# Writing out the order of three attention batches between an expert's matmul steps, and moving half of the query copies to ScalarE

## The chip, the core and the metric

The kernel runs on one NeuronCore of a Trainium2 chip. The core has a matrix engine (TensorE, "PE" in the profile, with its weight loads as "PEld"), a vector engine (VectorE, "DVE"), a scalar engine (ScalarE, "ACT"), a general-purpose engine (GpSimd, "POOL") and a sync engine ("SP") that here only issues transfers. [...] Matmul results land in PSUM, which the kernel uses as eight banks; everything else lies in SBUF. The metric is the time of one execution on the device, in microseconds; smaller is better.

## The reference

Two layers follow each other.

1. Attention with sorted blocks: batch 4, 8 heads, 768 positions, head size 64. A small matrix per head, 8 by 8, is normalised five times by rows and columns (Sinkhorn); it mixes the eight blocks of 96 keys and the eight blocks of 96 values. Each block of 96 queries then attends to its own mixed block.

```python
k_sorted = einsum('bhij,bhjcd->bhicd', P, k_b)
v_sorted = einsum('bhij,bhjcd->bhicd', P, v_b)
scores = scale * q_b @ k_sorted^T          # per block of 96
attn = softmax(scores)
x = attn @ v_sorted                        # laid out as 3072 tokens of 512
```

2. A layer of eight experts over all 3072 tokens. The logits `x @ w_gate` are made into a routing matrix P of 3072 by 8 by eight rounds of row and column normalisation over all tokens, and then

```python
for e in range(8):
    out += P[:, e:e+1] * (maximum(x @ w1[e], 0) @ w2[e])     # 512 -> 1024 -> 512
```

So no expert's output can be weighted before the logits of all four batches are there, but an expert's two matmuls need only the tokens that they multiply.

## The kernel before, in words

The span of 671.6 us has four stretches.

- **0 to 40 us**: the Sinkhorn matrices, and the attention of batch 0.
- **40 to 130 us**: the attention of batches 1, 2 and 3 (the loop of lines 515 to 543), each beside the dense first expert (`expert0`, line 418) of the batch ahead of it. This is the stretch that the change touches.
- **130 to 172 us**: the rest of expert 0 (`last_dense`), beside the routing's rounds (`balance`) and the first tiles of expert 1.
- **172 to 671 us**: experts 1 to 7, each by seven products in place of eight (Strassen), with sums of inputs, weights and hidden values made by GpSimd.

In the second stretch a batch is worked on by head pairs 0 to 3 (`hp`), in steps named by a letter:

- `q` (`queries`): six (twelve in batch 1) transposes of a pair's queries into one PSUM bank, then one copy of 128x768 to SBUF. Batch 1 transposes 64 columns at a time from `qt` (line 171); batches 2 and 3 first have GpSimd put a pair's queries side by side (`qr`, line 176, two buffers) and transpose 128 columns at a time (line 180). The copy is line 184 (ScalarE, batch 0) or line 186 (VectorE, batches 1 to 3).
- `k` (`keys`): the block mixing of the keys as matmuls (line 196) into two banks, and two VectorE copies (line 202).
- `s` (`scores`): 16 matmuls (line 220) into four banks, and four exponentials on ScalarE (line 234).
- `d` (`sums`): the softmax denominators by matmuls with ones (line 302) into two banks; the reciprocal is made on ScalarE by a logarithm (line 305) and an exponential (line 307).
- `m` (`mix`): attention times values (line 315) into two banks, and on VectorE the product with the reciprocal into the token tile `xtT` (line 318).
- `l` (`logits`): the gate's logits of the batch (line 331), `l0` for three of the four contraction blocks, `l3` for the last, then a copy into `glog` (line 335).

`sort_values` mixes the values of the batch: eight matmuls (line 147), eight copies (line 149, ScalarE and VectorE by turns) and eight transfers through which the mixed values change partitions (line 158, SP and GpSimd queues by turns). It is a generator that stops after every second head.

`expert0` is also a generator. A hidden step is four matmuls of 384 columns (line 397) and a rectifier on ScalarE (line 403) or VectorE (line 400). Half of an output tile is four matmuls of 512 columns (line 410); after the second half the tile is copied out (line 415), by ScalarE for tiles below 6 and by VectorE above. Batch 0 has 20 such steps left in this stretch, batches 1 and 2 have 28 each (8 hidden, 6 output, 8 hidden, 6 output).

What sets the order: TensorE's instructions are pinned to the order in which the program writes them. `weave(a, b, na, nb)` writes them by taking `na` visits to the attention generator and spreading `nb` expert steps between them evenly. The copies and other work of ScalarE, VectorE and GpSimd are mostly not pinned in batches 1 to 3; a scheduler places them on their engine when the program is built. The transfers of the next batch's `v`, `k`, `q` (line 80, GpSimd queue), the building of its mixing matrix `Rt` (line 134), and in batch 2 the load of expert 1's `w1` (line 89) and its sums (line 440) are pinned in the order of GpSimd.

All PSUM tiles of this stretch come from one pool of eight banks (`pa`, line 511), tag "bank". Buffers that hold several visits' work: `qTs` 4, `kTs` 3, `atp` 12 (three pairs' exponentials; in batch 1 the fourth pair uses the `qr` buffers), `recip` six slots in `osbl`.

Of the kernel before, what the change touches and what calls it, by code (L numbers as in the profile page):

```python
# [20 lines left out]
def mkap(t, dims, off=0):  # L21
    return bass.AP(tensor=t.tensor, offset=t.offset + off, ap=dims)
# [3 lines left out]
def kernel(  # L26
# [11 lines left out]
    nc = tc.nc  # L38
    B, H, S, D = 4, 8, 768, 64
# [19 lines left out]
    pin = tc.keep_in_program_order  # L59
# [12 lines left out]
    def load_batch(bb, parts):  # L72
        for d, name in ((vt, "vt"), (kt, "kt"), (qt, "qt")):
            d[bb] = kvp.tile([128, 8, 384], BF16, name=name, bufs=2)
        load_rest(bb, parts)

    def load_rest(bb, parts):
        for x, l0, n in parts:
            d, src = {"v": (vt, v), "k": (kt, k), "q": (qt, q)}[x]
            pin(nc.gpsimd.dma_start(  # L80
                out=d[bb][:, l0:l0 + n, :],
                in_=src[bb, l0:l0 + n].rearrange("h (p kk) d -> p h (kk d)", kk=6)))
# [4 lines left out]
    def load_w1(e):  # L87
        w1t[e] = wp.tile([128, 4, F], BF16, name="w1e")
        pin(nc.gpsimd.dma_start(out=w1t[e],
                                in_=moe_w1[e].rearrange("(kk k) f -> k kk f", k=128)))  # L90
# [39 lines left out]
    def build_r(bb, eng, n):  # L130

        Rt[bb] = perp.tile([128, 8, 8, 16], BF16, name=f"R{bb % 2}")
        for h in range(0, 8, n):
            ins = eng.tensor_tensor(
                out=mkap(Rt[bb], [Rt[bb].ap[0], [16, 8 * n], [1, 16]], off=h * 128),
                in0=mkap(Pb, [Pb.ap[0], [1, 8 * n], [0, 16]], off=(bb * 8 + h) * 8),
                in1=mkap(mask16, [mask16.ap[0], [0, 8 * n], [1, 16]]),
                op=ALU.mult)
            if eng is nc.gpsimd:
                pin(ins)  # L140
            yield


    def sort_values(bb, bank, n=8, h0=0):
        for h in range(h0, n):
            vps = bank([128, 384], F32)
            pin(nc.tensor.matmul(vps, Rt[bb][:, h].rearrange("p i c -> p (i c)"),  # L147
                                 vt[bb][:, h, :], start=True, stop=True))
            (nc.vector.tensor_copy if bb == 0 and h in (3, 5, 7) or bb and h % 2 else
             nc.scalar.copy)(  # L150
                vs[:, :, h, 0:64], vps.rearrange("p (kk d) -> p kk d", d=64))
            if h % 2:
                yield

        for i in range(NB if n == 8 else 0):
            eng = ((nc.sync, nc.gpsimd, nc.scalar)[i % 3] if bb == 0 else
                   nc.gpsimd if i % 2 else nc.sync)
            (pin if bb == 0 else lambda ins: ins)(eng.dma_start(
                out=mkap(vsbt[bb % 2], [[VW, 96], [1, 520]], off=i * 520),
                in_=vs[16 * i:16 * i + 16].rearrange("p kk h d -> p kk (h d)")))  # L160

    qT, kT, og = {}, {}, {}

    def queries(bb, hp, bank):

        qps = bank([128, 6, 128], BF16)
        if bb < 2:

            for kk in range(6):
                for h in range(2):  # L170
                    pin(nc.tensor.matmul(qps[64 * h:64 * h + 64, kk, :],
                                         qt[bb][:, 2 * hp + h, kk * 64:kk * 64 + 64],
                                         Ibig, is_transpose=True, start=True, stop=True))
        else:
            qr = sp.tile([128, 6, 2, 64], BF16, name="qr", bufs=2)
            nc.gpsimd.tensor_copy(
                qr.rearrange("p kk h d -> p h kk d"),
                qt[bb][:, 2 * hp:2 * hp + 2].rearrange("p h (kk d) -> p h kk d", d=64))
            for kk in range(6):
                pin(nc.tensor.matmul(qps[:, kk, :], qr[:, kk].rearrange("p h d -> p (h d)"),  # L180
                                     Ibig, is_transpose=True, start=True, stop=True))
        qT[bb, hp] = sp.tile([128, 128, 6], BF16, name="qTs", bufs=4)
        if bb == 0:
            pin(nc.scalar.copy(qT[bb, hp], qps.rearrange("p kk c -> p c kk")))
        else:
            nc.vector.tensor_copy(qT[bb, hp], qps.rearrange("p kk c -> p c kk"))

    def keys(bb, hp, bank):

# [162 lines left out]
        for x in PLAN0.split():  # L352
            do[x[0]](*(int(c) for c in x[1:]))

    def attention(bb, bank):

        def step(what, hp):
            if what == "q":
                queries(bb, hp, bank)
            elif what == "k":  # L360
                keys(bb, hp, bank)
            elif what == "s":
                scores(bb, hp, bank)
            elif what == "l":
                logits(bb, bank, (0, 1, 2) if hp == 0 else (3,))
            else:
                for b in range(2):
                    (sums if what == "d" else mix)(bb, hp, b, bank)

        plan = ("q0,q1,k0 k1,s0,q2 k2,s1,q3 k3,s2 s3,d0 d1,m0 d2,m1 d3,m2 m3 l0 l3" if bb == 1 else  # L370
                "q0,q1,k0 q2,k1,s0 q3,k2,s1 d0,k3,s2 m0,d1 s3 m1,d2 m2,d3 m3 l0 l3")
        for some in plan.split():
            for x in some.split(","):
                step(x[0], int(x[1]))
            yield


    begun = {}

# [52 lines left out]
    def sum_w(e):  # L432
        wct[e] = (wcq if e % 2 == 0 else wcp).tile([128, 3, 2, F // 2], BF16, name="wc")
        for kk in range(2):
            a11, a21 = (w1t[e][:, kk, f:f + 512] for f in (0, 512))
            a12, a22 = (w1t[e][:, 2 + kk, f:f + 512] for f in (0, 512))
            s1, s2, s4 = (wct[e][:, j, kk, :] for j in range(3))
            for a, b, o, c in ((a21, a22, ALU.add, s1), (s1, a11, ALU.subtract, s2),
                               (a11, a21, ALU.subtract, a21), (a12, s2, ALU.subtract, s4)):
                pin(nc.gpsimd.tensor_tensor(out=c, in0=a, in1=b, op=o))  # L440
                yield

    with tc.tile_pool(name="ps0", bufs=7, space=bass.MemoryType.PSUM,
# [27 lines left out]
        for eng, i0, n in ((nc.vector.tensor_copy, 0, 5), (nc.scalar.copy, 5, 3)):  # L471
            (pin if i0 else lambda ins: ins)(
                eng(Prep[:, i0:i0 + n], mkap(P, [P.ap[0], [8, n], [1, 8], [0, 16]], off=i0 * 8)))
        queries(0, 3, bank0)
        warm(3)
        pbps = bank0([128, 8, 32], F32)
# [21 lines left out]

        first_attention(bank0, warm, tiles())

    def weave(a, b, na, nb):

        t = 0
        for i in range(na):
            next(a, 0)
            while t * na < (i + 1) * nb:
                next(b, 0)
                t += 1

    with ExitStack() as c2:  # L510
        pa = c2.enter_context(tc.tile_pool(name="pa", bufs=8, space=bass.MemoryType.PSUM,
                                           reuse_waits="tile"))
        bank1 = lambda shape, dt: pa.tile(shape, dt, name="bank", tag="bank")
        ebank = lambda: bank1([128, 512], F32)
        for bb in range(1, B):
            ex = expert0(bb - 1, ebank)
            at1, left = attention(bb, bank1), 26
            if bb == 1:
                left = 16
                for _ in sort_values(1, bank1):  # L520
                    next(ex)
            else:
                for _ in range(28 - left):
                    next(ex)
            last = 3 if bb + 1 < B else 0
            left -= last
            cut = (lambda k: {5: 4, 8: 6}[k]) if bb == 1 else lambda k: left * k // 12
            weave(at1, ex, 5, cut(5))
            if bb + 1 < B:
                if bb == 2:  # L530
                    load_w1(1)
                load_batch(bb + 1, [(x, 0, 8) for x in "vkq"])
                for _ in build_r(bb + 1, nc.gpsimd, 4):
                    pass
                if bb == 2:
                    for _ in sum_w(1):
                        pass
            weave(at1, ex, 3, cut(8) - cut(5))
            if bb + 1 < B:
                weave(sort_values(bb + 1, bank1), ex, 5, last)  # L540
            weave(at1, ex, 4, left - cut(8))
            for _ in ex:
                pass
    actx.close()
# [15 lines left out]
    def ring(x):  # L560
        tiles, at = rings[x], [0]

        def take():
            at[0] += 1
            return tiles[(at[0] - 1) % len(tiles)]
        return take

    bank, obank = ring("bk"), ring("oacc")
# [298 lines left out]
    for m, o in enumerate(ends):  # L867
        e, p, hT, _ = chunks[-1]
# [4 lines left out]
    for r in range(len(pairs) + 6):  # L873
        n, i = r // 4, r % 4
        if n < C:
            e, p, hT, s3 = chunks[n]
# [9 lines left out]
        k = r - 5  # L886
# [71 lines left out]
```

## Time and profile before

| what | value |
|---|---|
| time, median of 3 runs | 672.5 us (671.78 to 672.51) |
| the profiled execution's own time | 673.45 us |
| its span | 671.6 us |
| TensorE busy | 654.9 us (98%) |
| VectorE, ScalarE, GpSimd busy | 478.9, 380.5, 469.7 us |
| mean granted TensorE clock | 0.997 |
| stretch of batch 1 / 2 / 3 | 41.0 to 66.7 / to 98.7 / to 130.3 us |

The profiled execution took 1.85 us more than its span from the first to the last instruction, and 0.95 us more than the median of the runs. "Busy" is the share of time in which at least one instruction of the engine ran. TensorE's matmuls are pipelined and their ends are modelled, so that its idle time in the profile is a lower bound: small gaps at a change of matmul shape lie inside the modelled ends and are better read from the distance of two starts.

A row of the timeline or of the chain begins with a start in us and a length in us; "x16" is the number of instructions merged in it, and brackets hold the idle time of the engine ahead of it and what ended that time. A row of the waits reads: waiting engine and line, what it waited for, us in total, number of times, longest.

### The profile page before, as it was taken

What the parts mean: (1) busy time and instruction counts of PE and PEld (TensorE: products, weight loads), DVE (VectorE), ACT (ScalarE), POOL (GpSimd) and SP (SyncE); (2) the same over time, 40 slices, a digit from 0 to 9 for tenths busy, and PEclk for the clock granted to TensorE, in tenths of its full rate; (3) what the DMA queues carried; (4) which work ended last, traced back from release to release, by engine and by line L of the source; (5) the groups of instructions that cost most, each with busy time, mean ns of one, the idle gap of its engine ahead of it and who ended that gap; (6) DMA issues with size and microseconds to landing.
All of it is one profiled execution on the core that took longest, in us unless ns stands there. A gap on an engine that the chain in (4) does not pass through costs nothing.

```text
span 671.6 us, 13230 instructions
## 1 busy us (share of the span) xinstructions
PE 654.9 (98%) x5094; PEld 427.3 (64%) x5094; DVE 478.9 (71%) x928; ACT 380.5 (57%) x748; POOL 469.7 (70%) x438
## 2 busy tenths in 40 slices
PE   5999999999999999999999999999999999999997
PEld 2665655554566666666666666666666666666665
DVE  6673768567677777777777777777777777777775
ACT  4567646467777755555555545555555555555540
POOL 3542741086979998779796979789787979836641
PEclk9899999999999999999999999999999999999999
DMA  9999873003040312030403040211203040000224
GB/s 155 178 212 152 139 115 59 6 1 64 0 64 8 57 18 47 1 64 1 63 2 62 1 63 2 42 22 18 47 1 63 1 63 1 1 1 33 95 82 171
DMA packets 32128, 36.58 MB, mean 54 GB/s; under 512 B 2048, under 2 KB 24672, under 8 KB 32064
## 3 DMA queue, kind: packets, MB, share of 16 engines
q0 software_dynamic: 25840, 27.72, 26.1%
q1 hardware_dynamic: 5712, 7.42, 3.6%
q8 instruction: 40, 0.66, 0.4%
q10 hardware_dynamic: 512, 0.59, 0.3%
q14 instruction: 24, 0.20, 0.1%
HBM read 52.45 MB, written 6.29 MB: 87 GB/s over the span
## 4 chain that ended last, share of the span: by engine, by line
PE 93%; DVE 3%; DMA 1%; ACT 1%; issue 1%; SPq 0%; ACTq 0%
PE bk L656 37%; PE oacc L767 37%; PE bank L410 5%; PE bank L397 4%; DMA vsb<-vs 1%; PE oacc L839 1%; PE bk L733 1%; PE bank L220 1%; PE bk L831 1%; PE bank L315 1%; PE bank L196 1%; PE bank L147 1%; PE bk L839 1%; DVE osbl L717 0%; PE bank L302 0%
## 5 line engine op out<-in xcount | busy, mean ns | idle before, releaser
L717 DVE SCALAR_TENSOR_TENSOR osbl<-oacc,glog,osbl 128x256 f32<-128x256 f32 (+1 forms) x411 | 219.2, 534 | 126.0 <-PE oacc L767 116.8
L642 ACT ACTIVATE hT<-bk 128x512 bf16<-128x512 f32 (+1 forms) x176 | 104.2, 592 | 149.6 <-PE bk L656 127.9
L656 PE MATMUL bk<-xtT,w1e 128*128 128x512 bf16 x504 | 149.1, 379 | 0.0
L767 PEld LDWEIGHTS <-hs 128*128 128x128 bf16 x984 | 96.3, 98 | 62.9 <-issue 0.3
L767 PEld LDWEIGHTS <-hT 128*128 128x128 bf16 x904 | 88.4, 98 | 58.3 <-issue 1.1
L757 POOL TENSOR_TENSOR hs<-hT 128x512 bf16<-128x512 bf16 x82 | 94.7, 1155 | 37.3 <-DVE hT L645 31.9
L767 PE MATMUL oacc<-w2e,hT 128*128 128x256 bf16 x764 | 114.6, 273 | 0.4 <-DVE osbl L717 0.3
L757 POOL TENSOR_TENSOR hs<-hs,hT 128x512 bf16<-128x512 bf16 x82 | 94.7, 1154 | 6.4
L656 PE MATMUL bk<-xc,wc 128*128 128x512 bf16 x336 | 99.1, 379 | 0.1
L757 POOL TENSOR_TENSOR hs<-hT,hs 128x512 bf16<-128x512 bf16 x82 | 94.5, 1153 | 6.4
L767 PE MATMUL oacc<-w2e,hs 128*128 128x256 bf16 x616 | 92.4, 273 | 0.0
L656 PEld LDWEIGHTS <-w1e 128*128 128x128 bf16 x672 | 65.8, 98 | 11.5 <-issue 0.3
L645 DVE CUSTOM_DVE_ANT_0 hT<-bk,p 128x512 bf16<-128x512 f32 x84 | 58.1, 691 | 7.7 <-PE bk L656 3.1
L691 ACT COPY p<-bk 128x512 f32<-128x512 f32 x84 | 49.2, 585 | 24.8 <-PE bk L656 24.7
L685 ACT COPY u<-bk 128x512 f32<-128x512 f32 x84 | 49.2, 585 | 22.2 <-PE bk L656 22.1
L676 ACT COPY bk<-bk 128x512 f32<-128x512 f32 x84 | 48.0, 572 | 20.5 <-PE bk L656 20.5
L645 DVE CUSTOM_DVE_ANT_0 hT<-bk,u 128x512 bf16<-128x512 f32 x84 | 57.0, 678 | 1.1 <-PE bk L656 0.6
L767 PE MATMUL oacc<-w2s,hs 128*128 128x256 bf16 x368 | 55.2, 273 | 0.0
L656 PEld LDWEIGHTS <-wc 128*128 128x128 bf16 x504 | 49.3, 98 | 8.0 <-issue 0.2
L710 DVE SCALAR_TENSOR_TENSOR s<-bk,hT 128x512 bf16<-128x512 f32 x80 | 54.4, 680 | 0.0
L656 PE MATMUL bk<-xc,w1e 128*128 128x512 bf16 x168 | 50.0, 379 | 0.0
L656 PE MATMUL bk<-xtT,wc 128*128 128x512 bf16 x168 | 50.0, 379 | 0.0
(158 smaller groups left out, 845.8 us busy)
## 6 DMA issues: line engine op xcount, KB each, us to landing
w2e<-in_moe_w_dram POOLq DMA_DIRECT2D x8, 1024.0 KB, 8.9
w1e<-in_moe_w_dram POOLq DMA_DIRECT2D x7, 1024.0 KB, 8.0
out_dram<-osbl SPq DMA_DIRECT2D x21, 256.0 KB, 2.0
vt<-in_v_dram POOLq DMA_DIRECT2D x3, 768.0 KB, 11.4
qt<-in_q_dram POOLq DMA_DIRECT2D x4, 384.0 KB, 10.1
kt<-in_k_dram POOLq DMA_DIRECT2D x4, 384.0 KB, 11.9
kt<-in_k_dram POOLq DMA_DIRECT2D x2, 768.0 KB, 13.9
qt<-in_q_dram POOLq DMA_DIRECT2D x2, 768.0 KB, 16.8
```

Source lines behind the costliest of these rows:

```text
L397: pin(nc.tensor.matmul(hps[:, 0:n], w1t[0][:, kk, fb * 128:(fb + 1) * 128], xtT[:, kk, c0:c0 + n], start=(kk == 0), stop=(kk == 3)))
L410: pin(nc.tensor.matmul(oacc, hTs[:, fb, tt * 128:(tt + 1) * 128], w2t[0][:, fb, :], start=(fb == 0), stop=(fb == 7)))
L642: relu = lambda o, x: nc.scalar.activation(out=o, in_=x, func=AF.Relu)
L645: return nc.vector._custom_dve(TENSOR_ADD_SAT, out=o, in0=x, in1=y, s0=TOP, s1=0.0)
L656: pin(nc.tensor.matmul(ps, wa[:, kk, :], xa[:, kk, :], start=(first and kk == 0), stop=(kk == 1), skip_group_check=True))
L676: pin(nc.scalar.copy(t["w"], t["u"]))
L685: pin(nc.scalar.copy(t["u2"], t["u"]))
L691: pin(nc.scalar.copy(t["p5"], t["v"]))
L710: pin(nc.vector.scalar_tensor_tensor(out=s3[:, i, :], in0=t["w"], scalar=0.0, in1=c12, op0=ALU.max, op1=ALU.subtract))
L717: pin(nc.vector.scalar_tensor_tensor(out=o, in0=ps, scalar=glog[:, t, e:e + 1], in1=o, op0=ALU.mult, op1=ALU.add))
L757: pin(nc.gpsimd.tensor_tensor(out=s[:, c], in0=a, in1=b, op=o))
L767: pin(nc.tensor.matmul(ps, h[:, fb, :], w[:, fb, :], start=(first and fb == 0), stop=(fb == 3), skip_group_check=True))
```

## The change: what it does

- `weave` and its counts go. Each of the batches 1 to 3 has a written list (`PLANS`): a token such as `q2,s0,k2` is one visit to attention, a number is so many expert steps, `v` is one stop of `sort_values`, `L` starts the next batch's loads (with the `Rt` build, and in batch 2 with `w1` of expert 1 and its sums).
- The visits are grouped otherwise. Batches 2 and 3 had nine visits with attention steps (`q0,q1,k0` / `q2,k1,s0` / `q3,k2,s1` / `d0,k3,s2` / `m0,d1` / `s3` / `m1,d2` / `m2,d3` / `m3`), now they have seven (`q0,q1,k0,k1` / `q2,q3,s0,k2` / `d0,s1,k3` / `m0,d1,s2` / `m1,d2,s3` / `m2,d3` / `m3`), with one to five expert steps between them. Batch 1 had nine, now eight. The logits come with fewer expert steps behind them: in batch 3 two after `l3` in place of four.
- The next batch's values (`v`) come later or are spread otherwise: in batch 1 from after `d3,m1`, in batch 2 from after `m2,d3`.
- In batches 1 to 3 the query copies of pairs 0 and 1 go to ScalarE, those of pairs 2 and 3 stay on VectorE.

The work itself, its amounts, shapes and buffers stay.

```diff
-        if bb == 0:
-            pin(nc.scalar.copy(qT[bb, hp], qps.rearrange("p kk c -> p c kk")))
-        else:
-            nc.vector.tensor_copy(qT[bb, hp], qps.rearrange("p kk c -> p c kk"))
+        (pin if bb == 0 else lambda ins: ins)(
+            (nc.scalar.copy if bb == 0 or hp < 2 else nc.vector.tensor_copy)(
+                qT[bb, hp], qps.rearrange("p kk c -> p c kk")))
...
+    PLANS = {1: "v 1 v 1 v 1 v 1 v q0,q1,k0,k1 1 q2,s0,k2 1 q3,s1,k3 1 s2 1 s3,d0 L 2 d1,d2,m0 "
+                "2 d3,m1 v 1 v 1 v 1 v v m2,m3 2 l0 1 l3 2",
+             2: "1 q0,q1,k0,k1 3 q2,q3,s0,k2 4 d0,s1,k3 L 5 m0,d1,s2 5 m1,d2,s3 4 m2,d3 "
+                "1 v 1 v 1 v v v m3 1 l0 1 l3 1",
+             3: "1 q0,q1,k0,k1 3 q2,q3,s0,k2 4 d0,s1,k3 5 m0,d1,s2 5 m1,d2,s3 4 m2,d3 "
+                "2 m3 1 l0 1 l3 2"}
+
+    def load_next(bb):
+        if bb == 3:
+            load_w1(1)
+        load_batch(bb, [(x, 0, 8) for x in "vkq"])
+        for _ in build_r(bb, nc.gpsimd, 4):
+            pass
+        if bb == 3:
+            for _ in sum_w(1):
+                pass
...
+        def sorts():
+            for b in {1: (1, 2), 2: (3,), 3: ()}[bb]:
+                yield from sort_values(b, bank)
+                yield
...
-        plan = ("q0,q1,k0 k1,s0,q2 k2,s1,q3 k3,s2 s3,d0 d1,m0 d2,m1 d3,m2 m3 l0 l3" if bb == 1 else
-                "q0,q1,k0 q2,k1,s0 q3,k2,s1 d0,k3,s2 m0,d1 s3 m1,d2 m2,d3 m3 l0 l3")
-        for some in plan.split():
-            for x in some.split(","):
-                step(x[0], int(x[1]))
-            yield
+        for x in PLANS[bb].split():
+            if x == "v":
+                next(values)
+            elif x == "L":
+                load_next(bb + 1)
+            elif x.isdigit():
+                for _ in range(int(x)):
+                    next(fill)
+            else:
+                for y in x.split(","):
+                    step(y[0], int(y[1]))
...
-            at1, left = attention(bb, bank1), 26
-            if bb == 1:
-                left = 16
-                for _ in sort_values(1, bank1):
-                    next(ex)
-            else:
-                for _ in range(28 - left):
-                    next(ex)
-            last = 3 if bb + 1 < B else 0
-            left -= last
-            cut = (lambda k: {5: 4, 8: 6}[k]) if bb == 1 else lambda k: left * k // 12
-            weave(at1, ex, 5, cut(5))
-            if bb + 1 < B:
-                if bb == 2:
-                    load_w1(1)
-                load_batch(bb + 1, [(x, 0, 8) for x in "vkq"])
...
-            weave(at1, ex, 3, cut(8) - cut(5))
-            if bb + 1 < B:
-                weave(sort_values(bb + 1, bank1), ex, 5, last)
-            weave(at1, ex, 4, left - cut(8))
+            attention(bb, bank1, ex)
             for _ in ex:
                 pass
```

More of the change, by code (lines that the diff above doesn't have):

```diff
@@ L353, in first_attention, with attention @@
             do[x[0]](*(int(c) for c in x[1:]))
-    def attention(bb, bank):
+    PLANS = {1: "v 1 v 1 v 1 v 1 v q0,q1,k0,k1 1 q2,s0,k2 1 q3,s1,k3 1 s2 1 s3,d0 L 2 d1,d2,m0 "
[5 rows of a table added]
+    def load_next(bb):
[7 more added lines that the diff above has]
+                pass
+    def attention(bb, bank, fill):
+        def sorts():
+            for b in {1: (1, 2), 2: (3,), 3: ()}[bb]:
+                yield from sort_values(b, bank)
+                yield
+        values = sorts()
         def step(what, hp):
@@ L499 @@
         first_attention(bank0, warm, tiles())
[L501 to L508, printed above, removed]
     with ExitStack() as c2:
@@ L516 @@
             ex = expert0(bb - 1, ebank)
-            at1, left = attention(bb, bank1), 26
-            if bb == 1:
-                left = 16
-                for _ in sort_values(1, bank1):
-                    next(ex)
-            else:
-                for _ in range(28 - left):
-                    next(ex)
-            last = 3 if bb + 1 < B else 0
-            left -= last
-            cut = (lambda k: {5: 4, 8: 6}[k]) if bb == 1 else lambda k: left * k // 12
-            weave(at1, ex, 5, cut(5))
-            if bb + 1 < B:
-                if bb == 2:
-                    load_w1(1)
-                load_batch(bb + 1, [(x, 0, 8) for x in "vkq"])
[L533 to L537, printed above, removed]
-            weave(at1, ex, 3, cut(8) - cut(5))
-            if bb + 1 < B:
-                weave(sort_values(bb + 1, bank1), ex, 5, last)
-            weave(at1, ex, 4, left - cut(8))
+            attention(bb, bank1, ex)
             for _ in ex:
```

## The prediction

> **What bounds the kernel now.** I read the page first, then the windows of the three batches, then who waited there, then the chain that ended last in batch 1. On the page TensorE is busy 98% of the span; the other engines stay at 57 to 71%.
>
> ```profile
> PE 654.9 (98%) x5094; PEld 427.3 (64%) x5094; DVE 478.9 (71%) x928; ACT 380.5 (57%) x748; POOL 469.7 (70%) x438
> ```
>
> So a new order can gain no more than TensorE's idle time in the stretch that it touches, and the gaps at its changes of shape. The windows of batches 1, 2 and 3 (length first, then each engine's busy time):
>
> ```profile
> 41.00:66.70 25.70, 24.18 (x324) 13.86 (x319) 14.77 (x28) 17.80 (x43) 10.61 (x15) 1.00 1.04 177
> 66.70:98.70 32.00, 31.98 (x361) 18.45 (x360) 21.10 (x38) 18.68 (x45) 19.73 (x22) 1.00 0.81 129
> 98.70:130.30 31.60, 30.83 (x353) 17.68 (x352) 23.20 (x41) 16.69 (x41) 2.67 (x4) 1.00 0.24 40
> ```
>
> TensorE idles 1.52, 0.02 and 0.77 us, at full granted clock (1.00). The waits name the places: two in batch 1, and one of 0.8 us as the next stretch starts.
>
> ```profile
> PE bank L220 <- DVE kTs L202: 1.0, 1, 1.0
> ...
> PE bk L831 <- DVE osbl L415: 0.8, 1, 0.8
> ...
> PE bank L315 <- DVE xtT L318: 0.5, 1, 0.5
> ```
>
> The chain through batch 1 shows what stands behind the first two. VectorE copies two pairs' queries, then the first keys, and only then can the first scores start; later the chain runs through ScalarE:
>
> ```profile
> 41.09 1.73 DVE qTs L186 x2
> 42.82 0.96 DVE kTs L202 x2
> 43.78 0.04 issue
> 43.83 0.56 PE bank L220 x16
> ...
> 49.00 0.81 ACT atp L234 x2
> ...
> 50.11 1.65 ACT qr L234 x4
> 51.76 0.76 ACT osbl L305 x2
> 52.52 0.41 ACT osbl L307
> 52.93 0.02 issue
> 52.95 0.57 DVE xtT L318
> ```
>
> From 46.40 to 59.50 ScalarE is busy 12.89 of 13.10 us: in the middle of batch 1 it is as full as TensorE. That decides how much of the idle time can go.
>
> **The change part by part.**
>
> *Query copies.* Six copies of 0.946 us (L186) leave VectorE, six of 0.777 us (the same form on ScalarE, L184) arrive there. In batch 1 ScalarE is free from 40.42 to 44.30 but for one rectifier of 0.49 us, so 1.55 us fit; if that cover were gone, all of it would lie on the full stretch behind. In batches 2 and 3 ScalarE is busy 17.1 of 22 us (70 to 92 us); 1.55 us more fit. VectorE's key copies then start at 41.5, not 42.74; the first pair's are done at 42.6, and the first scores come, after `q0,q1` (0.69 us), `k0,k1` (0.78), a hidden step (0.76) and `q2` (0.46), at 43.1. The wait of **0.99 us** goes.
>
> *Changes of shape.* The array works in three forms here: full (128x128: expert, values, `q` in batches 2 and 3), column halves (128x64 and 96x64: `k`, `d`, `m`, `q` in batch 1), row halves (64x96: `s`). Their prices come from starts in the timeline. Eight matmuls of 384 columns take 1.31 us from start to start with the same form behind them, 0.164 each, so 0.33 us for `k`, `s`, `d` or `m`. With another form behind: full to column 1.40 (+0.09); column to row 0.43 to 0.46 (+0.10 to 0.13); row to full 0.49 (+0.16); column to full 0.42 to 0.46 (+0.09 to 0.13); row to column 0.49 (+0.16); full to row 0.97 against 0.87 (+0.10). Batch 1 has 22 such changes and will have 21, batches 2 and 3 have 21 and will have 19: the savings are one column run less in batch 1 (0.21) and one column-to-row neighbour lost (0.09), and in batches 2 and 3 two row-to-column neighbours each (0.10 apiece, as 0.16 replaces 0.16 + 0.10). Together 0.12 + 0.20 + 0.20, **0.5 us**. [...]
>
> *Batch 1 behind the first scores.* The wait of **0.49 us** for a `mix` result goes too: `m0` moves behind two more expert steps. But ScalarE must still do some 16 us without a break: twelve exponentials at 0.37 us apart, four `d` at 1.56, a rectifier, two or three output copies at 0.48, the values' copies at 0.4. PSUM's eight banks go round, the ninth tile waiting for the reader of the first (217 tiles are made in this pool, so the last has bank 0, and the profile has the next stretch's first tile wait for just its copy). I walked the new list in those steps. Each tile finds its bank free but for four places: `s2` at 47.0 waits 0.05 for the copy of `q3`; the second bank of `d0` 0.1 for an exponential of `s2`; the output tile behind it 0.2 for the last one; and the fourth value matmul, at 56.7, 0.3 for the first logarithm of `d3`, which ScalarE begins at 56.4, after the output copies. **New waits 0.6 us.** Bounds: 0 if ScalarE runs as much earlier as its queue starts earlier (its first free moment, 43.6, is 0.7 us earlier than now), and 2.0 if an output copy is put behind two `d` on ScalarE, as now at 56.29 for a tile ready near 54.9. I take the walk, nearer to zero, since today's tighter order costs 0.49.
>
> *Batches 2 and 3.* `q2,q3,s0,k2` and the visits behind need all eight banks in 1.7 us; three to five expert steps (2.1 to 4.3 us) lie between visits, and the tightest, the second hidden step after `k2`, wants its bank 0.0 us after `q3`'s copy is done. Nothing, or 0.1 each; I take 0. GpSimd's `qr` copies: the second buffer for batch 2 is filled at 64.6 now, behind four transfer issues (61.62, 2.15 us); `q1` will want it at 66.5. `q2` and `q3` come in one visit; their `qr` copies (0.8 us each) wait for `q0` and `q1` and have 3.0 us from there. Covered by 1.5 us.
>
> *Moved transfers.* `L` starts in batch 1 with the issue of `v` at 43.16, right behind the four `vsb` issues on that queue, wherever the list has it; it lands 9.4 us later, 52.6, and the first value matmul comes at 55.2 (now 55.61). In batch 2 it stands behind the `qr` copies, `v` lands 11.9 us after 70.99 and is wanted near 89. SP's half of the `vsb` transfers only waits for the value copies and is used a batch later. Nothing. The load of expert 1's `w2` (L94) waits for a score matmul of batch 3, at 110.04; that visit comes some 5 us later, the load takes 8.9, so 124 in place of 119, and GpSimd first reads it at 137.07: 13 us cover.
>
> *The end.* `l3` and `m3` of batch 3 come closer to the end: 1.75 us of expert steps lie behind `l3`, and 4.4 us behind `m3`. The routing's first maximum (L612, 0.35 us) now ends 4.5 us ahead of its matmul at 131.72, later 2.7 us. Nothing, and the 0.8 us wait of L831 stays, as the last tile is the same one.
>
> Sum: 0.99 + 0.49 + 0.5 - 0.6 = 1.4 us gained. The profiled execution of 673.45 would be 672.05; it lies 0.95 above the median, so against the median of 672.5 I expect **671.1 us**. What this kernel's measurement can tell from no change is about 0.2%, 1.35 us, so the forecast lies on that edge.
>
> **The rivals.**
>
> *ScalarE holds nothing up* (the lower bound of the new waits): 0.99 + 0.49 + 0.5 is 2.0 us, 670.5. For it: its queue in batch 1 starts 0.7 us earlier, and expert steps lie between the `d` steps. Against: 12.89 of 13.10 us busy.
>
> *The stall only moves*: an output copy lands behind two `d`, 2.0 us at the bank of `d3`, in place of 0.6; gain 0 at 672.5. For it: the copy at 56.29 today. Against: in the new list that copy is written ahead of `d1`.
>
> *Slower: GpSimd puts the next loads ahead of the `qr` copies in batch 2.* `L` stands directly behind the third visit now, `q2,q3` in the second. If the scheduler writes the four issues (0.79, 0.92, 0.90, 0.91 us) and the two `Rt` builds (2.12) ahead of the `qr` copies for pairs 2 and 3, these come 5.6 us later, 1.5 of which are covered; `q2` then stalls TensorE 4.1 us, and the time is 672.5 - 1.4 + 4.1 = 675.2. It decides from a delay of 4.3 us on (1.5 of cover, the 1.4 gained, 1.35 to be told). For it: GpSimd's work isn't pinned against TensorE's, and in batch 1 the same issues run ahead of everything. Against: now they wait behind the two `qr` copies (68.67, then 70.21), though GpSimd had been idle for 4 us before.
>
> That the change doesn't do what it says is no rival here: the copies' engine and TensorE's order are written in the code.
>
> **How the numbers follow.** Forecast 48%, ScalarE harmless 22%, stall moved 12%, slower 18% (also for smaller delays of `qr` with a loss at TensorE that I cannot place). The forecast's own range is 670.6 to 671.8, by the waits of 0 to 1.2 us and a switch price of 0.09 to 0.16. A gain above 0.2% takes 28 of its 48, and all of the second: 50% faster; 20 and 12: 32% the same; 18% slower. The range of 669.9 to 673.5 reaches from the second case with the higher switch price (0.8 us in place of 0.5) and 0.3 for the runs' spread, to a `qr` delay half as long as in the slow case; it leaves out some 17%.
>
> **What would show it.** Right: no wait of L220 for L202 at the start of batch 1; ScalarE's chain without a break from 46 to 58 with 0.3 to 1 us of TensorE waiting for banks; L656 starting 1.4 us earlier, and nothing else changed behind. Wrong: a wait of L180 for `qr` in batch 2 or 3; TensorE waiting for an output copy of L415; or a gain in batches 2 and 3 well off 0.2 us each, which would say that the switch prices are not what the starts show.

## The result, and the profile after

The changed kernel takes 669.03 us (median of 5 runs, 668.02 to 670.27) against 672.5 us: 0.9947 of the time, with a 95% interval of 0.9923 to 0.9971. It is faster by about 3.5 us, 0.5%. The forecast was 671.1 us in a range of 669.9 to 673.5: the direction was right, the size was not, and the time lies below the range.

The profiled execution took 669.03 us with a span of 667.2 us. The page's engine line:

```profile
PE 650.2 (97%) x5017; PEld 427.1 (64%) x5094; DVE 473.9 (71%) x922; ACT 384.3 (58%) x754; POOL 469.8 (70%) x438
```

TensorE makes 5094 weight loads in both programs; 77 records of matmuls are missing from this trace, so its 97% is a little low.

(The line numbers shift with the edit: scores are L219, keys L195 and their copies L201, query copies L184, hidden steps L424 with rectifiers L427 and L430, expert outputs L437 with copies L442, denominators L301 with L304 and L306, mix L314 with its product L317, the next stretch's first matmuls L825.)

Three landmarks cut the stretch into the three batches: the first query transpose of batch 1, the first hidden step of the next `expert0`, and the first matmul of the next stretch. The windows between them, of the kernel before and of the changed one (length, then busy time of each engine):

```profile
40.43:66.74 26.31, 24.79 (x338) 14.44 (x338) 15.25 (x29) 17.80 (x43) 10.61 (x15) 1.00 1.04 178
66.74:98.71 31.97, 31.95 (x361) 18.45 (x360) 21.10 (x38) 18.68 (x45) 19.73 (x22) 1.00 0.82 129
98.71:130.33 31.62, 30.82 (x354) 17.68 (x352) 23.20 (x41) 16.69 (x41) 2.67 (x4) 1.00 0.24 40
```

```profile
39.87:64.28 24.41, 24.14 (x334) 14.10 (x337) 13.45 (x27) 19.05 (x45) 10.61 (x15) 1.00 1.13 197
64.28:96.03 31.75, 31.43 (x357) 18.50 (x360) 19.39 (x36) 20.06 (x47) 19.79 (x22) 1.00 0.74 121
96.03:126.47 30.44, 30.12 (x349) 17.71 (x352) 20.66 (x38) 17.94 (x43) 2.67 (x4) 1.00 0.33 55
```

Batch 1 fell by 1.90 us, batch 2 by 0.22, batch 3 by 1.18: 3.30 us in all. From the next stretch's first matmul to the start of the last matmul of the program both take 536.66 us, so nothing moved behind. The two spans differ by 4.35 us; the other 1.05 lie ahead of batch 1 (0.56) and behind the start of the last matmul (0.49), where the change edits nothing.

The profile names no wait for a bank or a copy any more in the stretch (smaller ones that it doesn't name come below). This is all that TensorE's waits show between 39 and 127 us of the changed kernel:

```profile
PE bank L437 <- issue: 0.3, 2, 0.2
```

The chain through the first half of batch 1 now runs through TensorE where VectorE's copies stood, and turns to ScalarE at 47 us as it did before at 49:

```profile
41.41 0.76 PE bank L424 x4
42.16 0.46 PE bank L171 x12
42.62 0.49 PE bank L219 x16
43.11 0.46 PE bank L195 x12
...
48.70 1.52 ACT qr L233 x4
50.22 0.76 ACT osbl L304 x2
50.98 0.80 ACT osbl L306 x2
51.78 0.47 ACT osbl L442
52.26 0.77 ACT osbl L304 x2
```

So two things call for a cause: batch 1 gained 1.90 us where the sum had 1.00 (0.99 + 0.49 + 0.12 - 0.6), and batch 3 gained 1.18 where the sum had 0.20. Batch 2 came out at the size predicted.

### The profile page after: what moved, and what is told of

Its sections match the earlier page's. It is cut to its first block, busy times and chain, and to the rows that moved or that the text cites. A ratio compares the mean times of both kernels' runs of the same rounds, so it can differ in the third digit from the quotient of the medians.

```text
span 667.2 us, 13154 instructions
## 1 busy us (share of the span) xinstructions
PE 650.2 (97%) x5017; PEld 427.1 (64%) x5094; DVE 473.9 (71%) x922; ACT 384.3 (58%) x754; POOL 469.8 (70%) x438
## 4 chain that ended last, share of the span: by engine, by line
PE 88%; POOL 4%; DMA 2%; issue 2%; ACT 2%; DVE 1%; POOLq 0%; ACTq 0%
PE oacc L761 37%; PE bk L650 34%; PE bank L424 5%; PE bank L437 4%; POOL hs L751 1%; DMA w1e<-in_moe_w_dram 1%; DMA qt<-in_q_dram 1%; POOL wc L467 1%; PE bk L727 1%; PE bank L219 1%; PE bk L825 1%; PE bank L195 1%; PE bank L314 1%; PE bank L147 1%; PE bk L833 1%
## 5 line engine op out<-in xcount | busy, mean ns | idle before, releaser
L650 PE MATMUL bk<-xtT,w1e 128*128 128x512 bf16 x478 | 143.5, 379 | 0.9
L650 PE MATMUL bk<-xc,wc 128*128 128x512 bf16 x317 | 95.2, 379 | 0.1
L650 PE MATMUL bk<-xtT,wc 128*128 128x512 bf16 x160 | 48.2, 379 | 0.4
L650 PE MATMUL bk<-xc,w1e 128*128 128x512 bf16 x158 | 47.8, 379 | 0.0
```

The source lines that it names most:

```text
L650: pin(nc.tensor.matmul(ps, wa[:, kk, :], xa[:, kk, :], start=(first and kk == 0), stop=(kk == 1), skip_group_check=True))
```

## Experiments

The lengths of the three batches between the landmarks repeat from profile to profile to within 0.02 us where the stretch is the same (batch 2 of the old order is 31.97 or 31.98 in five profiles). They are the measure below; the time of a run is too coarse for most of these questions, since what lies ahead of batch 1 varies (its first transpose came between 37.98 and 43.19 us). ring, split, before_relief, after_relief, before_relu and no_exp ran once each, and for these only the lengths are read.

Where a wait is not named, it is read from the distance between the start of one group of matmuls and the start of the next, compared with the same group where nothing holds it up. Such distances are those of the matmuls' own starts, unless the text says that they are those of the weight loads, which came 0.00 to 0.22 us ahead at the groups' starts in batch 1 of both kernels.

| kernel | batch 1 | batch 2 | batch 3 | together |
|---|---|---|---|---|
| before | 26.31 | 31.97 | 31.62 | 89.90 |
| changed | 24.41 | 31.75 | 30.44 | 86.60 |
| before_rot | 26.31 | 31.98 | 30.67 | 88.96 |
| after_last | 24.41 | 31.75 | 31.39 | 87.54 |
| copies_only | 25.34 | 31.89 | 30.58 | 87.81 |
| order_only | 25.19 | 32.04 | 30.74 | 87.97 |
| ring | 24.80 | 31.74 | 30.45 | 86.99 |
| split | 24.41 | 33.11 | 31.81 | 89.33 |
| all_act | 24.81 | 31.75 | 30.45 | 87.00 |
| before_relief | 26.30 | 31.97 | 30.67 | 88.94 |
| after_relief | 24.15 | 31.74 | 30.44 | 86.34 |
| before_relu | 26.42 | 31.97 | 30.68 | 89.07 |
| no_exp | 25.61 | 31.98 | 31.62 | 89.21 |
| fewer | 24.73 | 31.62 | 30.33 | 86.69 |
| best_visits | 24.42 | 31.62 | 30.33 | 86.37 |
| best_relief | 24.16 | 31.62 | 30.33 | 86.11 |
| best_relu | 24.09 | 31.62 | 30.33 | 86.05 |

### The wait at the end of batch 3: before_rot and after_last

In the old program the last expert tile of batch 3 lies in PSUM bank 0, and `bk0`, the next stretch's first tile, in bank 0 as well. In the changed program, which makes the same 217 tiles, the last one lies in bank 7. The banks do not simply go round: the last six tiles are in 4, 5, 7, 3, 6, 0 before and in 0, 4, 1, 5, 2, 7 after.

before_rot takes the coincidence out of the old kernel:

```diff
-             for x, n in (("bk", 5), ("oacc", 3))}
+             for x, n in (("oacc", 3), ("bk", 5))}
```

> The old kernel with one thing changed: the eight PSUM tiles of the next stretch are laid out in another order, so that the first one used (bk0) lies in bank 3 and no longer in bank 0, which the last expert tile of batch 3 still holds. Theory that the 0.8 us went by the luck of the banks: the stretch of batch 3, from its first hidden step to the next stretch's first matmul, falls from 31.62 to 30.8 us, batches 1 and 2 stay at 26.31 and 31.97, and the time falls by 0.8 us. Rival, that the new order itself took the wait away (two expert steps behind the logits in place of four): the stretch stays at 31.6.

after_last puts it into the new one:

```diff
+    ours = rings["bk"] + rings["oacc"]
+    rings = {"bk": ours[7:] + ours[0:4], "oacc": ours[4:7]}
```

> The new kernel with the reverse: its last expert tile lies in bank 7, and here the first tile of the next stretch is put into bank 7. Luck of the banks: the next stretch's first matmul waits for the last copy, batch 3 grows from 30.44 to 31.2 us (+0.8), the time by 0.8 us. Rival, that the order took the wait away: 30.4, no change.

Batch 3 fell from 31.62 to 30.67 in the one and rose from 30.44 to 31.39 in the other: 0.95 us each way, and nothing else moved. In time, before_rot is at 0.9989 (0.9977 to 1.0000) of the kernel before, and after_last at 0.9960 (0.9945 to 0.9974). TensorE's timeline at the border, before_rot first, then after_last (where the first tile goes by the name oacc2):

```profile
124.14 3.61 PE L410 MATMUL bank<-w2e,hTs 128*128 128x512 bf16 x16
127.59 1.46 PE L831 MATMUL bk<-xtT,w1e 128*128 128x384 bf16 x8
```

```profile
123.86 1.89 PE L437 MATMUL bank<-w2e,hTs 128*128 128x512 bf16 x7
126.53 0.81 PE L827 MATMUL oacc<-xtT,w1e 128*128 128x384 bf16 x4 [0.78 <-DVE osbl L442]
```

The wait comes and goes with the bank alone. The logits' place in the list has no part in it. It is worth 0.95 us where the profile names 0.78, since the named wait counts from the modelled end of the last tile's matmuls: in before_rot that end is at 124.14 + 3.61 = 127.75 us, and the next tile's first matmul starts at 127.59, 0.16 ahead of it. Of the 1.18 us that batch 3 gained, 0.95 is this luck and 0.23 is left for the visits and the copies.

### The two halves of the change: copies_only and order_only

copies_only is the old order with the first two pairs' query copies on ScalarE:

```diff
         if bb == 0:
             pin(nc.scalar.copy(qT[bb, hp], qps.rearrange("p kk c -> p c kk")))
+        elif hp < 2:
+            nc.scalar.copy(qT[bb, hp], qps.rearrange("p kk c -> p c kk"))
         else:
```

> The old kernel with only the query copies of pairs 0 and 1 on ScalarE, the old order of TensorE. If the copies alone remove the wait of the first scores for the keys (0.99 us), batch 1 falls from 26.31 to 25.3. If ScalarE, full from 46.4 to 59.5 in the old order, pays for its 1.55 us later, batch 1 stays near 26.3. Batch 2 stays within 0.2 of 31.97; batch 3's end may lose its 0.8 us wait, as the last tile now lies in bank 3.

order_only is the new order with these copies on VectorE:

```diff
-            (nc.scalar.copy if bb == 0 or hp < 2 else nc.vector.tensor_copy)(
+            (nc.scalar.copy if bb == 0 else nc.vector.tensor_copy)(
```

> The new kernel with all query copies of batches 1 to 3 back on VectorE, the new order. If the copies were what removed the first wait, batch 1 grows from 24.41 by 1.0 to 1.4 us (the four key copies behind two query copies, the first scores at 44.0 in place of 42.6), batches 2 and 3 by at most 0.2 each. If the order alone was enough, batch 1 stays at 24.4.

The copies alone take 0.97 us from batch 1: the first scores follow the second key step without a gap (0.45 us from start to start, 1.52 in the old kernel), and 0.09 come back at the second scores (0.58 in place of 0.49). The new order alone takes 1.12, and leaves most of that wait standing (1.19 us from the step ahead of the first scores to these, 0.73 more than undisturbed). TensorE's timeline of copies_only (scores are L222) and of order_only:

```profile
41.91 0.53 PE L198 MATMUL bank<-R,kt 128*64 128x128 bf16 x12
42.36 0.56 PE L222 MATMUL bank<-qTs,kTs 64*96 64x96 bf16 x16
```

```profile
41.90 0.53 PE L171 MATMUL bank<-Ibig,qt 128*64 128x128 bf16 x12
43.09 0.56 PE L219 MATMUL bank<-qTs,kTs 64*96 64x96 bf16 x16 [0.66 <-DVE kTs L201]
```

Two more things were not expected. In order_only batches 2 and 3 are 0.29 and 0.30 us longer than in the changed kernel: there the grouped visits need the copies' move (the key step `k2` behind the first scores takes 0.75 us in place of 0.46), and without it batch 2 would have come out 0.07 us worse than before. And the two halves give 0.97 + 1.12 = 2.09 us apart in batch 1, 1.90 together: the order takes 0.33 of the first wait by itself, and the copies would have taken that, too.

In batches 2 and 3 the copies alone gain 0.08 and 0.09 us, though no visit is moved. In the old kernel the key step ahead of the first scores takes 0.55 and 0.54 us in these batches, and 0.46 in copies_only: a small wait that nothing names, and that goes with the copies. The new order brings one of its own in return: by the weight loads' starts the scores of pair 2 take 0.56 us in both batches, where all others take 0.49.

As times: copies_only 0.9959 (0.9946 to 0.9973) of the kernel before, order_only 0.9985 (0.9971 to 0.9999). In both the last tile lies in another bank than `bk0`, so both contain the 0.95 us of the border.

### What a change of the array's form costs: split

The visits of batches 2 and 3 are taken apart (batch 2 shown), with `bk0` away from the last tile:

```diff
-             2: "1 q0,q1,k0,k1 3 q2,q3,s0,k2 4 d0,s1,k3 L 5 m0,d1,s2 5 m1,d2,s3 4 m2,d3 "
-                "1 v 1 v 1 v v v m3 1 l0 1 l3 1",
+             2: "1 q0,q1,k0 1 k1 2 q2,q3,s0 1 k2 3 d0 1 s1 1 k3 L 3 m0 1 d1 1 s2 3 m1 1 d2 1 s3 1 "
+                "m2 1 d3 1 v 1 v 1 v v v m3 1 l0 1 l3 1",
```

> The new kernel with the visits of batches 2 and 3 taken apart: single steps k, s, d, m between expert steps, the same number of expert steps in all; 32 changes of the array's form in each of these batches in place of 19, and the next stretch's tiles laid out so that no bank wait stands at the end. By the pair prices of the prediction (0.21 us for each column run set apart, 0.09 to 0.10 for each lost neighbour) each batch grows by 1.3 us, 2.6 in all. If the changes cost what the measured gain of batches 1 to 3 hints at beyond the waits (1.0 us for five changes, 0.2 each), each grows by 2.6, 5.2 in all. If the visits gain by something else, under 0.7 each.

Batches 2 and 3 grew by 1.36 and 1.37 us; the pair prices said 1.3. So 13 more changes of form cost 0.105 us each here (0.11 if the 0.07 us at the scores of pair 2 is counted, which take 0.49 us again in this kernel), and prices read from the starts in the timeline of one execution added up. Whether only the number of changes counts, or also which two forms meet, these runs do not tell.

### What held batch 1 at its d and m steps: before_relief, before_relu, no_exp

By the distances of starts, TensorE came late at more places in batch 1 of the old kernel than the profile names. This is its timeline there: three groups of 16 mix matmuls (L315), of which only the second shows a wait. To the start of what follows, the first takes 0.89 us by the weight loads' starts, the second 1.28, the third 0.60; by the matmuls' own starts 0.76, 1.12 and 0.44.

```profile
49.88 0.93 PE L302 MATMUL bank<-atp,one 96*64 96x384 bf16 x8
50.67 0.74 PE L315 MATMUL bank<-atp,vsb 96*64 96x96 bf16 x16
51.43 1.02 PE L410 MATMUL bank<-w2e,hTs 128*128 128x512 bf16 x4
52.38 0.52 PE L302 MATMUL bank<-atp,one 96*64 96x384 bf16 x4
52.73 0.34 PE L315 MATMUL bank<-atp,vsb 96*64 96x96 bf16 x8
53.56 0.36 PE L315 MATMUL bank<-atp,vsb 96*64 96x96 bf16 x8 [0.49 <-DVE xtT L318]
53.86 1.04 PE L410 MATMUL bank<-w2e,hTs 128*128 128x512 bf16 x4
54.82 0.52 PE L302 MATMUL bank<-qr,one 96*64 96x384 bf16 x4
55.17 0.51 PE L315 MATMUL bank<-atp,vsb 96*64 96x96 bf16 x16
```

The eight `d` matmuls ahead of the first group (L302, 49.88) took 0.79 us. In the changed kernel the same two groups take 0.67 and 0.44 us, and the `d` matmuls take 0.67 in before_relu, too:

```profile
50.60 0.84 PE L301 MATMUL bank<-atp,one 96*64 96x384 bf16 x8
51.28 0.51 PE L314 MATMUL bank<-atp,vsb 96*64 96x96 bf16 x16
51.72 1.04 PE L437 MATMUL bank<-w2e,hTs 128*128 128x512 bf16 x4
```

So TensorE waited 0.12 + 0.32 = 0.44 us at the first `d` and `m` of the old kernel, and 0.68 at the second `m`. before_relief takes the output copies off ScalarE, before_relu the rectifiers of the hidden steps, and no_exp leaves out the exponentials that make the reciprocals of batch 1:

```diff
-            (nc.scalar.copy if t < 6 else nc.vector.tensor_copy)(osbl[:, t, :], oacc)
+            nc.vector.tensor_copy(osbl[:, t, :], oacc)
```

> The old kernel with the six output copies of batch 1's stretch (tiles below 6, 0.48 us apart each on ScalarE) moved to VectorE, and nothing else. The distances of starts say that TensorE waits for some 2.3 us in batch 1 of the old kernel: 1.0 for the keys, and 1.3 in small pieces behind ScalarE, of which the profile names 0.5 as a wait. If so, batch 1 falls from 26.31 to between 25.0 and 25.4. If only the named 0.5 us hang on ScalarE, it falls to 25.8 at best.

```diff
-            if c0 and fb % 2:
+            if c0 == 384 or c0 and fb % 2:
```

> The old kernel with all rectifiers of the hidden steps beside batch 1 on VectorE, so that the one of 0.4 us that stands between the exponentials on ScalarE leaves its queue. If the starts that come late at the d and m steps of pairs 0 and 1 (0.89 and 1.28 us for 16 mix matmuls that take 0.60 two visits on) hang on ScalarE's queue of exponentials and logarithms, they shrink by 0.3 to 0.4 us together and batch 1 falls from 26.31 to 25.9 to 26.0. If they are the price of the matmuls' own change of form or tile, batch 1 stays at 26.3.

```diff
-        nc.scalar.activation(out=r, in_=r, func=AF.Exp, scale=-1.0)
+        if bb != 1:
+            nc.scalar.activation(out=r, in_=r, func=AF.Exp, scale=-1.0)
```

> The old kernel, but batch 1 leaves out the exponential that turns the logarithm of each denominator into its reciprocal (line 307; eight instructions, 3.1 us of ScalarE's queue from the first d on; the tokens of batch 1 are then scaled by the logarithm). If the late starts behind the first d (1.28 us for a group that takes 0.60 undisturbed, 1.12 and 1.04 for two that take 0.97) hang on ScalarE's queue, all three go: batch 1 falls from 26.31 by 0.9 to 25.4, while the 0.89 us ahead of them stay. If only the named 0.49 us hangs on it, batch 1 is at 25.8. If the change of form makes the distances, 26.3.

before_relief did nothing (26.30): the first output copy stands behind three pairs' logarithms on ScalarE (at 56.29 us in the kernel before, the logarithms at 51.59, 53.16 and 54.72), too late to be in the way of the first two `d` and `m`. before_relu missed its aim. VectorE, with more to do, was late with the last keys, the fourth scores started 0.37 us later, and ScalarE came to its first logarithm no earlier; batch 1 rose by 0.11. Still, the late scores were made up in part: by the weight loads' starts the first group fell from 0.89 to 0.68, and the eight `d` matmuls ahead of it from 0.58 to 0.52. So 0.27 us of the 0.44 there is shown to be a wait; the rest rests on the comparison with the changed kernel alone. no_exp is clean: batch 1 falls by 0.70, all of it at the second group, which now looks like the third.

```profile
50.83 0.52 PE L302 MATMUL bank<-atp,one 96*64 96x384 bf16 x4
51.18 0.51 PE L316 MATMUL bank<-atp,vsb 96*64 96x96 bf16 x16
51.62 1.04 PE L411 MATMUL bank<-w2e,hTs 128*128 128x512 bf16 x4
```

Its distance went from 1.28 to 0.60. The profile named 0.49 of the 0.68 us. The other two late starts of the expectation (1.12 and 1.04) stayed, so they are no wait for that queue, and 0.9 us was too much. They are no waits at all: by the matmuls' own starts these two expert groups take 0.96 and 0.95 us, and the one that had 0.97 by the weight loads takes 0.97.

### ScalarE's room in the new order: all_act and after_relief

all_act puts the other two query copies on ScalarE too:

```diff
-            (nc.scalar.copy if bb == 0 or hp < 2 else nc.vector.tensor_copy)(
+            nc.scalar.copy(
```

> The new kernel with all four query copies of batches 1 to 3 on ScalarE. If ScalarE is as full as TensorE in batch 1 (12.89 of 13.10 us before), two more copies of 0.78 us push it back by 1.55 us, and batch 1 grows from 24.41 by up to 1.5 us. If its fullness was only work that could as well wait, batch 1 grows by less than 0.3. Batches 2 and 3 stay within 0.2.

after_relief has the edit of before_relief, in the changed kernel.

> The new kernel with the same six copies on VectorE. If the predicted 0.6 us of new waits behind ScalarE are there, hidden in the modelled ends of matmuls (the first d of pair 0, 0.2, and two of the value matmuls, 0.2 each), batch 1 falls from 24.41 to 23.8 to 24.0. If ScalarE keeps nobody waiting in the new order, it stays at 24.4.

1.55 us more on ScalarE cost 0.40 us in batch 1, and nothing in batches 2 and 3. By the weight loads' starts the delay shows at the fourth scores (0.63 in place of 0.49) and at the first `d` (0.78 in place of 0.63). Taking the output copies away brought 0.26 us: the second pair of value matmuls fell from 0.60 to 0.38, while the first `d` fell from 0.63 to 0.52 and the expert tile behind it took 0.08 more. So in the new order ScalarE does hold TensorE a little at the values, though the waits list shows nothing there. At the first `d`, the other place where the walk of the prediction had put a wait, the output copies are not what holds it. In best_relu (below) the two steps ahead of it take 0.11 us more, and the first `d` 0.45 from start to start in place of 0.64: there is a wait, too, which later scores make up for.

### Banks in turn: ring

ring hands out the eight banks strictly in turn in batch 1, from a pool of its own, and leaves batches 2 and 3 as they are (the rest of the edit is left out):

```diff
...
+        made = [0]
+
+        def turn_bank(shape, dt):
+            made[0] += 1
+            return pr.tile(shape, dt, name="bank", tag=f"bank{(made[0] - 1) % 8}")
...
```

> The new kernel, but in batch 1 PSUM's eight banks are handed out strictly in turn, as the prediction had assumed; batches 2 and 3 as they are. If the predicted new waits of 0.6 us failed to come because a tile takes a bank that is already free instead of the ninth-last one, batch 1 grows from 24.41 to about 25.0 us with waits of TensorE for ScalarE's readers. Rival, that ScalarE is simply not late in the new order: batch 1 stays at 24.4 in either way of handing out. The first tiles of batch 2 may wait up to 0.5 us at the border of the two pools.

Batch 1 rose by 0.39 us, less than the 0.6 that I expected of it: by the weight loads' starts later by 0.10 at the second scores, by 0.25 at the second mix, by 0.17 at the first two pairs of values and by 0.05 at the expert tile behind the first `d`, earlier by 0.18 at this `d`. The scheduler's choice of a bank is thus worth 0.39 us over a strict turn, but the new order's waits do not all come from it or go with it. In batches 2 and 3 a strict turn can't be had: an output tile stays open across a visit that takes eight banks.

### Versions meant to beat both: fewer, best_visits, best_relief, best_relu

fewer puts the scores last in four visits (parts of the lines), and all four versions lay out the next stretch's tiles as before_rot does:

```diff
-... q2,s0,k2 1 q3,s1,k3 1 s2 ...
+... q2,k2,s0 1 q3,k3,s1 1 s2 ...
...
-... 4 d0,s1,k3 ...
+... 4 d0,k3,s1 ...
```

> A version meant to beat both: the new order, but in four visits the scores stand last (q2,k2,s0 and q3,k3,s1 in batch 1; d0,k3,s1 in batches 2 and 3), which takes two changes of form from batch 1 and one each from batches 2 and 3; the next stretch's tiles laid out so that no bank wait stands at the end. By the pair prices (0.26 to leave out a row-to-column and a column neighbour, against 0.16 and 0.12) 0.1 to 0.15 us per change, 0.5 in all: stretches 24.15, 31.6, 30.3, time 0.5 us less than the new kernel. Rival: the keys' copies come earlier and the scores later, so that s1 or s2 waits, and batch 1 grows instead.

In batches 2 and 3 it gave 0.13 and 0.11 us, as the prices said. In batch 1 the rival came true: the scores start 0.4 us later, ScalarE's queue with them, and the first `d` takes 1.10 us in place of 0.63 (weight loads' starts); the batch is 0.32 longer. So best_visits has the edit in batches 2 and 3 alone, best_relief adds the output copies on VectorE, best_relu the rectifiers as well.

> The new kernel with d0,k3,s1 in place of d0,s1,k3 in batches 2 and 3 only, batch 1 in the new kernel's order, and the next stretch's tiles laid out so that no bank wait stands at the end. From the run with fewer changes: batch 1 24.41, batch 2 31.62, batch 3 30.33, together 86.36 against 86.60, the time 0.24 us less than the new kernel's. If batch 1 depends on where the banks of batches 2 and 3 lie: up to 0.3 more.

> The version before this with the six output copies of batch 1 on VectorE as well. If both gains add: batch 1 23.9, batch 2 31.62, batch 3 30.33, together 85.85, 0.75 us less than the new kernel's stretch. If VectorE becomes late with the keys or queries of batch 1, that stretch stays at 24.4.

> The best version so far (visits with fewer changes in batches 2 and 3, output copies of batch 1 on VectorE) with the same rectifiers on VectorE. If ScalarE's queue is what still holds batch 1 (0.1 us left at the first d), it falls from 24.16 to 24.0 to 24.1. If VectorE, which now has both, is late with the keys or the queries of pairs 2 and 3, it grows by 0.1 to 0.5.

The stretches are 86.37, 86.11 and 86.05 us, against 86.60 of the changed kernel and 89.90 of the one before. As times, against the kernel before: fewer 667.83 us, 0.9935 (0.9922 to 0.9947); best_visits 669.01, 0.9959 (0.9939 to 0.9979); best_relief 668.31, 0.9937 (0.9915 to 0.9960); best_relu 668.47, 0.9943 (0.9928 to 0.9959). All four beat the kernel before. That they beat the changed one is told only by the stretch, by 0.2 to 0.55 us (and fewer not even by that): their intervals overlap with its own, 0.9923 to 0.9971.

## Why the prediction was wrong

The sum had 1.4 us. The stretch gained 3.30, and this is where the other 1.9 us was.

- **Query copies, 0.99 us: right.** copies_only gives 0.97, and order_only gets most of the wait back. That ScalarE pays nothing for them in batch 1 also held: in copies_only the groups at the first two `d` and `m` take as long as in the old kernel (the wait named there is 0.5 us in both).
- **Changes of shape, 0.5 us: right in price, with some luck in the gain.** Batch 2 gained 0.22 and batch 3 0.23 beside the border, 0.20 each were predicted; split confirmed the prices at 13 changes a batch (1.36 and 1.37 against 1.3). But copies_only shows that 0.08 and 0.09 of these gains are the copies', and the new order waits 0.07 in each batch, where the prediction had put nothing. The two nearly cancel, which leaves about 0.2 for the forms: the total came out right with two terms missing. A condition was missing, too: without the copies on ScalarE the new order loses 0.07 in these batches (order_only).
- **"The 0.8 us wait of L831 stays, as the last tile is the same one": wrong, by 0.95 us.** This is the larger of the two failed steps. The last tile is the same one, but its bank is not. I had taken "217 tiles, so the last has bank 0" from a ring of eight, because the one case in the profile fitted it. before_rot and after_last show the wait to hang on the bank alone, and it is worth 0.95 and not 0.78, as the named wait begins 0.16 late, at a modelled end.
- **The idle time of batch 1, 1.49 us: too small.** I read waits from TensorE's busy time and from the named waits, and the matmuls' modelled ends hide parts of them. The second wait was 0.68 and not 0.49 (no_exp), and 0.44 more lay unnamed at the first `d` and `m` (before_relu took 0.27 of it away). The key step ahead of the first scores took 1.52 us in the old order and 0.46 undisturbed, so the first wait was 1.06 and not 0.99.
- **New waits, 0.6 us: right in place, a little large.** By the starts the changed kernel waits 0.21 at the first `d` (0.63 against 0.42 for the price of four such matmuls and a change of form) and 0.22 at the values (0.60 against 0.38): 0.43. The profile names none of it. after_relief shows the part at the values to be there, and best_relu most of the part at the first `d`.

Together for batch 1: 0.12 for the forms, and 1.06 + 0.68 + 0.44 - 0.43 = 1.75 for waits, 1.87 of the measured 1.90. Of these, 0.17 us at the first `d` and `m` is read from starts alone, and no run shows what it waited for. The three rivals: ScalarE holding nothing up (670.5) was nearest in time, but for another reason; the stall that only moves did not come; GpSimd kept the `qr` copies ahead of the loads (in batch 2 the copies start at 65.56 us, the first issue at 67.11), and nothing of that rival was seen.

The range failed with the two steps: it was built on the bounds of the new waits and on a late `qr` copy, and had no term for a gain that the sum did not know of.

## What to carry to other kernels

Where waits are to be counted for an engine whose ends are modelled in the profile, compare the distance from start to start with a clean occurrence of the same group; the named waits of batch 1 gave 1.49 us where the starts gave 2.18. Use the matmuls' own starts for it: those of the weight loads showed two late groups here that were none (1.12 and 1.04 us, where the matmuls' own starts gave 0.96 and 0.95). The wait at the border of the two PSUM pools, 0.95 us, came and went here with the banks that the allocator happened to give, so look up the bank of the last tile and of the first one before calling such a wait fixed, and lay the next pool's tiles out so that its first tile is not in the bank that frees last. When the gain is under one per cent of the run, measure the length of the stretch between two landmarks in the profile: it repeated to 0.02 us here, where run times spread over 2 us and more.

## What the hardware showed that I had not expected

Batch 1's first transpose came between 37.98 and 43.19 us after the start in the 17 profiles of this study, though no edit touched what lies ahead of it. In four of them the mean granted TensorE clock from 27 to 38 us was 0.82 to 0.84 and not 1.00, and there it came at 40.43, 41.49, 41.81 and 43.19. With the clock at 1.00 it came between 37.98 and 40.02, but for ring (41.34), so the clock is not the only thing that moves it. The kernel before has such a case in the profile that the prediction was made from; from batch 1 on the clock was 1.00 in it as in the changed kernel.
